# Spacing out the indirect row transfers at the hand-over from attention to the expert tiles

## The chip, the cores and the metric

The kernel runs on one core of a Trainium2 chip. The metric is the device time of one execution in microseconds; the kernel before was timed three times, and its median is the time before. One further execution was profiled, and all views below are of that one.

## The reference

Two layers follow each other. The first is attention over 4 batches of 8 heads, 768 positions and 64 features. Keys are grouped into 24 chunks of 32. For each query an upper bound of its score with every chunk is formed from the chunk's elementwise minimum and maximum, the six causal chunks with the highest bounds are kept, and a softmax attention runs over the kept, causal keys alone. The second layer sends each of the 3072 resulting rows of 512 numbers to one of eight experts:

```
ub    = sum_d max(q_d * kmin_d, q_d * kmax_d)        # per query and chunk, causal
keep  = the 6 chunks with the largest ub
attn  = softmax(scale * q k^T, kept and causal) v     # -> x, 3072 x 512
e     = argmax(x w_gate);  g = softmax(x w_gate)[e]
out   = g * (relu(x w1[e]) w2[e])                     # w1: 512 x 1024, w2: 1024 x 512
```

## The kernel before

**Attention, pairs 0 to 15.** Two heads are worked on at a time, which makes sixteen pairs (`NP = 16`), four to a batch. A pair has seven units: `scores(i, u)` makes the scores of unit u on TensorE (L469) and their exponentials on ScalarE (L474) into a tile P, and `av(i, u)` multiplies them with the values (L497). P tiles that cross the diagonal are masked, by GpSimd with an affine select (L482), in the last pair by VectorE with a product (L479). The pairs overlap: while pair i is in its scores, pair i+1 gets its chunk bounds (`ub`, `bound`, `maxes`, `choose`, `mask`, `put`) and pair i+2 its transposes. `norm(i, half)` divides a finished half by the softmax sums on VectorE (L521 to L525) and writes the row block `xrow` and the head's share `lgt` of the gate logits; `lg_add` sums these.

**Routing, once per batch.** When a batch's four pairs are done, `logits`, `gate`, `rank` (twelve small matmuls, L576 to L582) and `rank_v` find every row's expert and its slot `sli` among that expert's rows. Six indirect transfers of 128 rows each (`scatter`, L602) then write the rows to `xs_dram`, sorted by expert. For batches 0 to 2 this happens inside the next batch's pairs, at the slots that `scatters(i, slot)` lists; the last batch's six follow after attention has ended.

**Expert tiles.** 28 tiles of 128 rows are computed on the ordinary path, each for one expert. For tile j, `gather(j)` (L708) is an indirect transfer of its 128 rows from `xs_dram`; `x_in(j)` (L720) is a DMA transpose, issued by the SyncE queue, that puts them into the layout TensorE needs; `up(j)` is 8 matmuls (L741) followed by ReLU on ScalarE (L749) and a DMA transpose of the hidden rows, hT (L753), again on the SyncE queue; `down(j)` is 8 matmuls (L797), scaled on ScalarE (L803); and `y_out` (L781) is an indirect transfer of the 128 finished rows to their places in `out`. The first eleven tiles (`NA = 11`) hold rows of batches 0 to 2 alone, so their gathers may run before the last batch's rows are written. A table of tiles, `table(True)` for these eleven and `table(False)` for the others, comes from VectorE.

**Order.** The orders on TensorE, GpSimd and, after the first pair, VectorE are written out by hand (`manual_schedule`); in the tile phase the SyncE order is too. What is written first is executed first on its engine, and an instruction that waits holds back all behind it on that engine. In the last pair, `early` issues gathers as the pair goes on, each held back by a small GpSimd copy into `paced` that waits for a P tile:

```
if i == NP - 2 and slot == 3:
    gather(0)
    gather(1)
if i == NP - 1:
    if slot < 4:
        nc.gpsimd.tensor_copy(out=paced[:], in_=st[i][f"P{(1, 3, 5, 6)[slot]}"][0:1, 0, 0:1])
    gather(2 + slot)
    x_in(slot)
```

In the tile phase the order at step j is: at most one gather of a later tile, `up(j)` with its hidden transpose, at most one `x_in` of a later tile, then `down(j - 2)` with its output transfer. TensorE so runs up(j), down(j-2), up(j+1), down(j-1), and so on. From j = 8 on, the gather in step j is that of tile j+5 and the `x_in` that of tile j+3.

Of the kernel before, what the change touches and what calls it, by code (L numbers as in the profile page):

```python
# [10 lines left out]
FP32 = mybir.dt.float32  # L11
BF16 = mybir.dt.bfloat16
I32 = mybir.dt.int32
AF = mybir.ActivationFunctionType
# [10 lines left out]
def kernel(  # L25
# [10 lines left out]
    nc = tc.nc  # L36
# [4 lines left out]
    NCH = S // CH  # L41
# [58 lines left out]
    wgb = const.tile([128, HP, 2 * E], FP32)  # L100
    tokid = const.tile([128, B, 2, 3], I32)
    warm = const.tile([128, 1], FP32)
    paced = const.tile([1, 1], FP32)
    KTE, QSB, KS, KD = [], [], [], []
    for i in range(3):
        KTE.append(buf.tile([128, 2, S], BF16, name=f"KTE{i}"))
# [144 lines left out]
    def prep_steps(i):  # L251
# [120 lines left out]
        def select_first(filler, idle, scored, between):  # L372
            v_t(0)
            v_t(1)
            pm = [ps_m.tile([64, 384], BF16, tag="m", name="pm") for _ in range(2)]

            def turn(hf):
                for t in range(3):
                    nc.tensor.transpose(pm[hf][:, ts(t, 128)],
                                        nsel[:, 3 * hf + t].rearrange("p a n -> p (a n)"), ident_b[:])  # L380

            def put(hf):
                for hd in range(2):
                    nc.vector.tensor_copy(out=qsb[64:64 + NCH, hd, ts(hf, 384)],
                                          in_=pm[hf][32 * hd:32 * hd + NCH, :])

            bound()
            maxes(0, 3)
            choose(0, 3)
            turn(0)  # L390
            v_c(0, act=True)
            v_c(1, act=True)
            maxes(3, 6)
            choose(3, 6)
            put(0)
            filler()
            idle(2)
            scored()
            turn(1)
            between()  # L400
            put(1)
# [24 lines left out]
        def maxes(lo, hi):  # L426
            for t in range(lo, hi):
                for hd in range(2):
                    nc.vector.max(out=s["top8"][:, t, hd], in_=s["ubm"][:, t, hd])

        def choose(lo, hi):
            u3 = s["ubm"][:].rearrange("p t a n -> p (t a) n")[:, 2 * lo:2 * hi]
            t3 = s["top8"][:].rearrange("p t a n -> p (t a) n")[:, 2 * lo:2 * hi, TOPK - 1:TOPK]
            nc.vector.tensor_tensor(nsel[:].rearrange("p t a n -> p (t a) n")[:, 2 * lo:2 * hi, 0:NCH], u3,
                                    t3.to_broadcast([128, 2 * (hi - lo), NCH]), ALU.is_lt)
# [92 lines left out]
    def lg_add(i):  # L528
        b, hp = divmod(i, HP)
        eng = nc.vector if i == NP - 1 else nc.gpsimd  # L530
        lg, lgt = bst[b]["lg"], st[i]["lgt"]
        if hp == 0:
            eng.tensor_tensor(lg[:], lgt[:, :, :, 0], lgt[:, :, :, 1], ALU.add)
        else:
            for hd in range(2):
                eng.tensor_tensor(lg[:], lg[:], lgt[:, :, :, hd], ALU.add)
# [277 lines left out]
    def weights(slot):  # L814
        for n in range(2 * NW):
            if 1 + n * 71 // (2 * NW - 1) == slot:
                load_w(order_w[n // 2], n % 2)

    def scatters(i, slot):
        b, hp = divmod(i, HP)  # L820
        todo = {(1, 1): (0,), (1, 3): (2,), (2, 1): (4,), (2, 3): (1,), (3, 1): (3,), (3, 3): (5,)}
        if b == B - 1:
            todo = {(1, 1): (0, 2), (1, 2): (4, 1), (1, 3): (3, 5)}
        if b > 0 and (hp, slot) in todo:
            route[b - 1]["scatter"](todo[hp, slot])

    def early(i, slot):
        if i == NP - 2 and slot == 3:
            gather(0)
            gather(1)  # L830
        if i == NP - 1:
            if slot < 4:
                nc.gpsimd.tensor_copy(out=paced[:], in_=st[i][f"P{(1, 3, 5, 6)[slot]}"][0:1, 0, 0:1])
            gather(2 + slot)
            x_in(slot)

    MAN = {PE, POOL}
    with tc.manual_schedule(engines=MAN):
# [5 lines left out]
        with tc.manual_schedule(engines={DVE, ACT}):  # L844
            idle = consts_first()
            p0, p, pj = prep[0], prep[1], prep[2]
            p0["first"](idle)
            load(1, "v")
            spread(1, "k")
            load(2, "k")  # L850
            spread(1, "q")
            load(2, "q")
            load(2, "v")
            consts_pool()
            consts_last()
            idle(2)

            def filler():
                p["k_t"](0)
                idle(3)  # L860

            p0["select_first"](filler, idle, lambda: scores(0, 0), lambda: p["k_red"](0))
            scores(0, 1)
            p["k_t"](1)
            spread(2, "k")
            load(3, "k")
            p["k_out"](0, 0)
            p["k_out"](0, 1)
            p0["vw"]()
            p["k_red"](1)  # L870
            p0["vw_c"]()
            scores(0, 2)
            p["k_out"](1, 0)
            p["k_out"](1, 1)
            p["q_t"](0)
            p["q_t"](1)
            spread(2, "q")
            load(3, "q")
            av(0, 0)
            p["kse"]()  # L880
            p["q_va"](0)
            p["q_v"](1)
            p["q_a"](0)
            p["q_a"](1)
            scores(0, 3)
            av(0, 1)
            p["ub"]()
            norm(0, 0)
            p["bound"]()
            p["maxes"](0, 6)  # L890
            p["choose"](0, 6)
            scores(0, 4)
            av(0, 2)
            p["q_c"](0)
            p["q_c"](1)
            p["q_d"](0)
            p["q_d"](1)
            weights(1)
            pj["k_t"](0)
            pj["k_t"](1)  # L900
            spread(3, "k")
            load(4, "k")
            scores(0, 5)
            pj["k_red"](0)
            pj["k_out"](0, 0)
            pj["k_out"](0, 1)
            av(0, 3)
            p["mask"]()
            p["put"]()
            scores(0, 6)  # L910
            weights(2)
            weights(3)
            p["v_t"](0)
            p["v_t"](1)
            p["v_c"](0, act=True)
            pj["k_red"](1)
            p["v_c"](1)
            pj["k_out"](1, 0)
            pj["k_out"](1, 1)
            mask_rows(1)  # L920
            av(0, 4)
            pj["q_t"](0)
            pj["q_t"](1)
            spread(3, "q")
            load(4, "q")
            pj["q_va"](0)
            pj["q_v"](1)
            pj["kse"]()
            mask_rows(2)
            av(0, 5)  # L930
            pj["q_a"](0)
            pj["q_a"](1)
            pj["q_s"](0)
            weights(4)
        dve = tc.manual_schedule(engines={DVE})
        dve.__enter__()
        for i in range(1, NP):
# [10 lines left out]
            norm(i - 1, 1)  # L948
            load(i + 2, "v")
            lg_add(i - 1)  # L950
            if i < NP - 1:
                scores(i, 0)
                scores(i, 1)
# [7 lines left out]
                pn["q_s"](1)  # L961
            weights(5 * i)
            scatters(i, 0)
            early(i, 0)

            if pj:
                pj["k_t"](0)
# [11 lines left out]
            spread(i + 3, "k")  # L979
            load(i + 4, "k")  # L980
            weights(5 * i + 1)

            av(i, 0)
            scores(i, 3)
# [63 lines left out]
        norm(NP - 1, 1)  # L1048
        lg_add(NP - 1)
        with tc.manual_schedule(engines={SP, POOL}):  # L1050
            gather(7)
            x_in(5)
            r["logits"]()
            tok(0)
            tok(1)
            r["gate"]()
            gather(8)
            up(1)
            x_in(6)
            tok(2)  # L1060
            tok(3)
            r["rank"]()
            r["rank_v"]()
            gather(9)
            up(2)
            x_in(7)
            r["scatter"]((0, 1))
            gather(10)
            down(0)
            tok(4)  # L1070
            tok(5)
            for _ in table(False):
                pass

            def tiles(lo, hi):
                for j in range(lo, hi + 2):
                    if lo == 0 and j < 3:
                        continue
                    if lo == 0 and j < 5:
                        r["scatter"](((2, 3), (4, 5))[j - 3])  # L1080
                    if lo == 0 and 6 <= j < hi - 5:
                        gather(j + 5)
                    if j < hi:
                        up(j)
                    if lo == 0 and (j < 6 or 8 <= j < hi - 3):
                        x_in(j + (5 if j < 6 else 3))
                    if lo == 0 and j + 3 < hi:
                        tok(j + 3)
                    if lo == 0 and j == hi + 1:
                        down_last()  # L1090
                    elif j - 2 >= lo:
                        down(j - 2, turn_last if lo == 0 and j == hi else None)

            tiles(0, JM)
        dve.__exit__(None, None, None)
# [47 lines left out]
```

The softmax here doesn't subtract the row's maximum and nothing guards it: scores larger than these inputs give would overflow.

## Time and profile before

| what | value |
|---|---|
| device time, three runs | 345.01, 348.87, 351.6 us; median 348.87 us |
| span of the profiled execution | 353.5 us |
| TensorE busy | 324.1 us, 92% of the span |
| GpSimd busy | 211.2 us, 60% |
| ScalarE busy, VectorE busy | 206.6 us and 179.1 us |
| row scatters L602, mean of one | 1043 ns |
| output scatters L781, mean of one | about 989 ns |
| gathers L708, mean of one | about 1050 ns |

The shares are averages over phases with different limits. Attention takes the first 243 us of the profiled span, and the tile phase, with the last batch's routing inside it, the rest. The mean of an indirect transfer is the time for which GpSimd is occupied by it; the rows move afterwards, on the DMA engines. In the windows view, the columns after the stretch and its length are busy times of TensorE matmul, TensorE weight load, VectorE, ScalarE and GpSimd with their instruction counts, then the granted TensorE clock as a share of full speed, the DMA engines' busy share, and the bytes that they moved in GB/s.

### The profile page before, as it was taken

The numbers are of one execution on the slowest core, as the hardware profiler recorded it, in microseconds if no ns is written. First come the engines' busy times: TensorE is split into PE (matmuls) and PEld (weight loads), VectorE is DVE, ScalarE is ACT, GpSimd is POOL, SyncE is SP. The second block draws the span as 40 slices with busy tenths as digits, with TensorE's granted clock in tenths as the row PEclk, the third lists the DMA queues.
The fourth block names the chain that finished last, engine by engine and source line by source line (L and its number), as shares of the span: only waits on it lengthen the run. The fifth ranks groups of instructions, "written<-read, shape, count | busy, mean of one in ns | idle before, by whom it ended". The sixth has DMA issues, their size and how long they took to land.

```text
span 353.5 us, 13417 instructions
## 1 busy us (share of the span) xinstructions
PE 324.1 (92%) x5333; PEld 241.7 (68%) x5333; DVE 179.1 (51%) x725; ACT 206.6 (58%) x353; POOL 211.2 (60%) x368
## 2 busy tenths in 40 slices
PE   7899988999999999999999969876999999999990
PEld 3589978989899998799898858662444444444440
DVE  7778675776975776965866946424600000000010
ACT  4677865966767867667867735431344544454540
POOL 8657364555487785597893585553655656554231
PEclk9999999999999999999999989997899999999997
DMA  8968979789799999799897766245899998998730
GB/s 183 222 144 165 242 139 189 151 168 198 161 176 222 204 179 216 150 186 223 161 222 111 130 125 119 54 99 120 179 196 228 213 209 191 210 205 173 202 95 23
DMA packets 107005, 59.93 MB, mean 170 GB/s; under 512 B 76219, under 2 KB 99773, under 8 KB 106944
## 3 DMA queue, kind: packets, MB, share of 16 engines
q0 software_dynamic: 18048, 29.42, 44.1%
q1 hardware_dynamic: 87296, 29.26, 38.0%
q8 instruction: 44, 0.72, 0.8%
q10 hardware_dynamic: 1600, 0.39, 0.5%
q14 instruction: 17, 0.14, 0.1%
HBM read 56.14 MB, written 10.51 MB: 189 GB/s over the span
## 4 chain that ended last, share of the span: by engine, by line
PE 62%; issue 11%; POOL 7%; DVE 6%; ACT 4%; DMA 3%; another core or an unknown queue 2%; SPq 1%; POOLq 0%; ACTq 0%; DVEq 0%
PE po L497 22%; PE ps L469 10%; PE ubp L416 6%; PE ph L741 5%; PE py L797 5%; POOL out_dram L781 3%; PE pt L259 3%; PE vwp L334 3%; PE pt L318 3%; PE pt L287 3%; ACT P L474 2%; DMA QSB<-xg 1%; DMA hT<-h__5430 1%; PE pm L440 1%
## 5 line engine op out<-in xcount | busy, mean ns | idle before, releaser
L474 ACT ACTIVATE P<-ps 128x768 f32<-128x768 f32 x144 | 88.0, 664 | 44.9 <-PE ps L469 35.4
L497 PE MATMUL po<-V,P 128*64 128x73 f32 x2688 | 106.1, 228 | 8.3 <-POOL P L482 2.9
L497 PEld LDWEIGHTS po<-V,P 128*64 128x64 f32 x2688 | 99.9, 137 | 16.2 <-issue 4.5
L469 PE MATMUL ps<-QSB,KTE 128*64 128x384 bf16 (+2 forms) x576 | 55.3, 296 | 0.6 <-ACT P L474 0.6
L482 POOL TENSOR_SCALAR_AFFINE_SELECT P<-P 128x256 f32<-128x256 f32 x90 | 34.6, 408 | 29.8 <-ACT P L474 29.4
L797 PE MATMUL py<-w_all,hT 128*128 x216 | 51.0, 379 | 0.5 <-DMA hT<-h__5430 0.5
L274 ACT ACTIVATE KTE<-pt 64x512 bf16<-64x512 f32 (+1 forms) x64 | 31.0, 485 | 22.9 <-DVE kmn L270 22.1
L199 POOL DMA_DIRECT2D w_all<-in_moe_w_dram x64 | 41.3, 646 | 0.1
L797 PEld LDWEIGHTS <-hT 128*128 128x128 bf16 x216 | 21.1, 98 | 26.1 <-DMA hT<-h__5430 0.9
L469 PEld LDWEIGHTS <-KTE 128*64 128x64 bf16 x576 | 28.7, 111 | 6.9 <-issue 5.8
L602 POOL DMA_INDIRECT xs_dram<-xrow,sli x21 | 21.9, 1043 | 18.9 <-DVE xrow L568 7.7
L741 PE MATMUL ph<-w_all,KTE 128*128 x120 | 31.1, 403 | 2.0 <-issue 1.9
L781 POOL DMA_INDIRECT out_dram<-V,ti x14 | 13.8, 989 | 18.4 <-ACT V L803 15.4
L741 PE MATMUL ph<-w_all,QSB 128*128 x104 | 24.6, 379 | 0.0
L416 PE MATMUL ubp<-KS,qT 128*64 128x48 f32 x384 | 24.1, 224 | 0.2
L741 PEld LDWEIGHTS <-KTE 128*128 128x128 bf16 x120 | 12.0, 101 | 17.9 <-issue 5.9
L416 PE MATMUL ubp<-KD,qA 128*64 128x48 f32 x384 | 23.7, 222 | 0.4 <-issue 0.4
L521 DVE RECIPROCAL rec<-po 128x6 f32<-128x6 f32 x32 | 6.2, 195 | 34.7 <-PE po L497 17.4
L416 PEld LDWEIGHTS ubp<-KS,qT 128*64 128x64 f32 x384 | 20.6, 137 | 3.1 <-PE pt L259 2.0
L444 DVE COPY QSB<-pm 24x768 bf16<-24x768 bf16 x30 | 16.5, 551 | 8.8 <-PE pm L440 8.1
L416 PEld LDWEIGHTS ubp<-KD,qA 128*64 128x64 f32 x384 | 20.5, 138 | 0.6 <-issue 0.6
L328 DVE COPY vT<-pt 128x384 f32<-128x384 f32 x29 | 15.9, 553 | 8.8 <-PE pt L318 8.7
(207 smaller groups left out, 503.5 us busy)
## 6 DMA issues: line engine op xcount, KB each, us to landing
w_all<-in_moe_w_dram POOLq DMA_DIRECT2D x64, 256.0 KB
V<-in_v_dram SPq DMA_DIRECT2D x32, 192.0 KB
w_all<-in_q_dram SPq DMA_DIRECT2D x30, 192.0 KB
k<-in_k_dram SPq DMA_DIRECT2D x15, 256.0 KB
k<-in_k_dram SPq DMA_DIRECT2D x15, 128.0 KB
xs_dram<-xrow,sli POOLq DMA_INDIRECT x21
out_dram<-V,ti POOLq DMA_INDIRECT x14
q<-in_q_dram ACTq DMA_DIRECT2D x2, 96.0 KB
```

The costliest lines, as they stand in the source:

```text
L199: d = nc.gpsimd.dma_start(out=dst, in_=src)
L274: nc.scalar.activation(kte[0:64, hd, ds(128 * lo, 128 * n)].rearrange("p (w s) -> p w s", s=n), s[f"kp{hf}"][64 * hd:64 * hd + 64, :].rear ...
L416: nc.tensor.matmul(pu[c:c + CW, 3 * hf + t].rearrange("p a n -> p (a n)"), lhsT=s[f"{nm}{hf}"][:, ds(t * 128 + c, CW)], rhs=w_[:], start=( ...
L444: nc.vector.tensor_copy(out=qsb[64:64 + NCH, hd, :], in_=s["pm"][32 * hd:32 * hd + NCH, :])
L469: nc.tensor.matmul(pv[c:c + CW, hd, :], lhsT=kte[:, hd, ds(kb * 128 + c, CW)], rhs=qsb[:, hd, ds(qb * 384 + 384 - w, w)], start=True, stop ...
L474: nc.scalar.activation(P[:, :, ds(c0, w)], pv, AF.Exp)
L482: nc.gpsimd.affine_select(out=pd, in_=pd, pattern=[[0, 2], [1, 128]], compare_op=ALU.is_ge, fill=0.0, base=0, channel_multiplier=-1)
L497: nc.tensor.matmul(po[c:c + CW, t].rearrange("p a d -> p (a d)")[:, ds(hd * VW, VW)], lhsT=P[:, hd, ds(col + c, CW)], rhs=vt[:, kb, ds((1 ...
L602: d = nc.gpsimd.indirect_dma_start(out=xs_dram[:], out_offset=bass.IndirectOffsetOnAxis(ap=sli[:, u:u + 1], axis=0), in_=bst[b][f"xrow{u % ...
L741: nc.tensor.matmul(ph[:, fh, :], lhsT=xT[:, c, :], rhs=w1_all[:, ds(wo + (c * F + fh * 512), 512)], start=(c == 0), stop=(c == NDC - 1), s ...
L781: d = nc.gpsimd.indirect_dma_start(out=out[:], out_offset=bass.IndirectOffsetOnAxis(ap=ti[:], axis=0), in_=y, in_offset=None, bounds_check ...
L797: nc.tensor.matmul(py[:], lhsT=hT[:, c, :], rhs=w2_all[:, ds(wo + c * DM, DM)], start=(c == 0), stop=(c == NFC - 1))
```

## The change

Indirect transfers on GpSimd are spread out so that in the written order at most two follow each other in the last three pairs and around the first tiles. What stands between them is other GpSimd work or, where there is none, memsets of a small tile (`rest_a_while`, three memsets of 1 x 256 numbers).

- The scatters of batch 2 go from two to a slot in pair 13 to one at each of six slots over pairs 13 and 14.
- `gather(0)` stays at the end of pair 14, `gather(1)` goes to the start of pair 15; the later early gathers are each held back by a copy (`behind`) that waits for a tile of pair 15, then a memset. `gather(6)` waits for the second half of pair 15's logits.
- After attention, gathers 6 and 7 come ahead of the last batch's scatters, gather 8 after the first output, gathers 9 and later in the steps j = 5 and on. So the gather of step j is that of tile j+4 (before: j+5), and `x_in` there is that of tile j+3 for j = 4 and 5 and of tile j+2 from j = 7 on (before: j+3 from j = 8 on).
- On TensorE `up(2)` moves ahead of the last batch's `rank`.
- Near the start, one of two mask copies of the first pair moves from VectorE to ScalarE, `put(0)` ahead of `choose(3, 6)`, and two filler matmuls are dropped; in the same prologue `av(0, 4)` and one reduction move ahead of the value transposes.

```
-    paced = const.tile([1, 1], FP32)
+    paced = const.tile([1, 256], FP32)
...
-                for hd in range(2):
-                    nc.vector.tensor_copy(out=qsb[64:64 + NCH, hd, ts(hf, 384)],
-                                          in_=pm[hf][32 * hd:32 * hd + NCH, :])
+                nc.vector.tensor_copy(out=qsb[64:64 + NCH, 0, ts(hf, 384)], in_=pm[hf][0:NCH, :])
+                nc.scalar.activation(qsb[64:64 + NCH, 1, ts(hf, 384)], pm[hf][32:32 + NCH, :], AF.Copy)
...
+            put(0)
             choose(3, 6)
-            put(0)
             filler()
-            idle(2)
+            idle(1)
...
         if b == B - 1:
-            todo = {(1, 1): (0, 2), (1, 2): (4, 1), (1, 3): (3, 5)}
+            todo = {(1, 1): (0,), (1, 2): (2,), (1, 3): (4,), (2, 0): (1,), (2, 1): (3,), (2, 2): (5,)}
...
+    def rest_a_while(n=3):
+        for _ in range(n):
+            nc.gpsimd.memset(paced[:], 0.0)
+
+    def behind(ap):
+        nc.gpsimd.tensor_copy(out=paced[:, 0:1], in_=ap)
+        rest_a_while(1)
+
     def early(i, slot):
         if i == NP - 2 and slot == 3:
+            rest_a_while(1)
             gather(0)
-            gather(1)
         if i == NP - 1:
+            s = st[i]
+            if slot == 0:
+                behind(s["P2"][0:1, 0, 0:1])
+            if slot == 1:
+                behind(s["lgt"][0:1, 0, 0, 0, 0:1])
+            if slot == 2:
+                behind(s["P5"][0:1, 0, 0:1])
+            if slot == 3:
+                behind(s["P6"][0:1, 0, 0:1])
             if slot < 4:
-                nc.gpsimd.tensor_copy(out=paced[:], in_=st[i][f"P{(1, 3, 5, 6)[slot]}"][0:1, 0, 0:1])
-            gather(2 + slot)
+                gather(2 + slot)
             x_in(slot)
...
-                idle(3)
+                idle(2)
...
+            av(0, 4)
+            pj["k_red"](1)
             p["v_t"](0)
             p["v_t"](1)
             p["v_c"](0, act=True)
-            pj["k_red"](1)
...
-            av(0, 4)
...
             lg_add(i - 1)
+            if i == NP - 1:
+                gather(1)
...
             scatters(i, 0)
-            early(i, 0)
...
             weights(5 * i + 1)
+            early(i, 0)
...
         with tc.manual_schedule(engines={SP, POOL}):
+            behind(st[NP - 1]["lgt"][0:1, 0, 1, 0, 0:1])
+            gather(6)
+            rest_a_while()
             gather(7)
+            rest_a_while()
             x_in(5)
             r["logits"]()
             tok(0)
             tok(1)
             r["gate"]()
-            gather(8)
             up(1)
             x_in(6)
             tok(2)
             tok(3)
+            up(2)
             r["rank"]()
             r["rank_v"]()
-            gather(9)
-            up(2)
-            x_in(7)
             r["scatter"]((0, 1))
-            gather(10)
+            rest_a_while()
             down(0)
             tok(4)
             tok(5)
+            gather(8)
+            rest_a_while()
...
                         r["scatter"](((2, 3), (4, 5))[j - 3])
-                    if lo == 0 and 6 <= j < hi - 5:
-                        gather(j + 5)
+                        rest_a_while()
+                    if lo == 0 and 5 <= j < hi - 4:
+                        gather(j + 4)
                     if j < hi:
                         up(j)
-                    if lo == 0 and (j < 6 or 8 <= j < hi - 3):
-                        x_in(j + (5 if j < 6 else 3))
-                    if lo == 0 and j + 3 < hi:
-                        tok(j + 3)
+                    if lo == 0 and (j in (4, 5) or 7 <= j < hi - 2):
+                        x_in(j + (3 if j < 6 else 2))
+                    if lo == 0 and (j < 6 or 7 <= j < hi - 2):
+                        tok(j + (3 if j < 6 else 2))
                     if lo == 0 and j == hi + 1:
                         down_last()
                     elif j - 2 >= lo:
                         down(j - 2, turn_last if lo == 0 and j == hi else None)
+                    if lo == 0 and j < 5:
+                        rest_a_while()
```

## The prediction

> **What bounds the kernel now.** I read the page's busy shares first, then the chain of waits, then the windows of the stages that it named, then each engine's timeline there.
>
> ```profile
> PE 324.1 (92%) x5333; PEld 241.7 (68%) x5333; DVE 179.1 (51%) x725; ACT 206.6 (58%) x353; POOL 211.2 (60%) x368
> ...
> PEclk9999999999999999999999989997899999999997
> ```
>
> TensorE is the bound, so only its pauses and slow clock can be won: 353.5 - 324.1 = 29 us idle. The clock dips in two slices. The chain has one step of unknown releaser, at the hand-over:
>
> ```profile
> 234.02 0.76 DVE P L479 x2
> 234.78 8.36 another core or an unknown queue
> 243.16 0.21 DVE rec L521
> ...
> 246.44 3.48 PE ph L741 x8
> 249.91 1.73 PE py L797 x8
> ...
> 291.08 4.28 DMA QSB<-xg
> ```
>
> The reciprocal at 243.16 needs the end of attention's products, which should come soon after 235. The timelines of TensorE and GpSimd show what lies between:
>
> ```profile
> 235.06 2.45 PE L497 MATMUL po<-V,P 128*64 128x73 f32 x59
> 237.83 0.36 PE L497 MATMUL po<-V,P 128*64 128x73 f32 x3 [0.33 <-issue]
> 238.54 0.38 PE L497 MATMUL po<-V,P 128*64 128x73 f32 x4 [0.35 <-issue]
> ```
> ```profile
> 235.69 1.02 POOL L708 DMA_INDIRECT xg<-xs_dram,grow  x1 [0.16 <-issue]
> 237.01 1.01 POOL L708 DMA_INDIRECT xg<-xs_dram,grow  x1 [0.30 <-issue]
> ...
> 239.63 1.00 POOL L708 DMA_INDIRECT more_x<-xs_dram,grow  x1 [0.30 <-issue]
> ```
>
> TensorE pauses with "issue", waiting for nothing visible, while six gathers follow each other on GpSimd from 234.15 on. Its 72 last products take 5.2 us (235.06 to 240.3), against 2.4 for the same 72 a pair earlier. The count reaches VectorE at 243.14, about when the row of gathers is over. I read this as the indirect transfers holding back TensorE's issue and its counts; it is a coincidence in time so far, not shown. The same signs are smaller elsewhere: two gathers at 222.85 and 224.26 (24 value products spread over 1.94 us, elsewhere 0.66), and the six of 252.65 to 259.06, after which a ScalarE step of tile 2 stood idle 3.81 us.
>
> The last phase has no slack:
>
> ```profile
> 268.00:289.00 21.00, 21.00 (x99) 9.50 (x97) 0.96 (x6) 9.93 (x13) 12.28 (x12) 1.00 1.00 214
> ```
>
> TensorE is busy all 21.00 us, and the DMA engines too (share 1.00). Eight matmuls of `up` or `down` take 1.73 us.
>
> **What the Trainium skill says.** "TensorE: Matmul & The Clock Gate", Part 1: after an idle window of about 3.4 us the clock halves until about 3.4 us of activity. The trace agrees: 0.50 in 243 to 249, where `up(2)` takes 3.48 instead of 1.73 us. "Perfetto Trace Analysis", DMA Instruction — SWDGE (GPSIMD): the instruction ends when its descriptors are written, not when data has moved. It agrees: a gather occupies GpSimd 1.0 us and lands about 3.3 after issue. "DMA: Bandwidth & Descriptors", Issuing engines are not separate DMA queues: all issuers share 16 engines[...]. No page I read says that indirect transfers in a row hold back TensorE.
>
> **The change part by part: gains.**
>
> *Start.* Two idle matmuls of 0.216 us go: -0.4. The split of the mask copies (0.5 us) over two engines is what lets them go, so I count it with them. `av(0, 4)` ahead of the value transposes only swaps TensorE's own work: nothing.
>
> *A, scatters of pair 13.*
>
> ```profile
> 209.30 1.73 PE L497 MATMUL po<-V,P 128*64 128x73 f32 x24 [2.67 <-POOL P L482]
> ```
>
> Its products wait 2.67 us at 209.30 for a GpSimd mask that stood behind two scatters (206.44, 207.80), and run at clock 0.50 in 209 to 212 (24 in 1.73). One scatter less ahead is 1.0 + 0.30 = 1.3; a shorter wait may keep the clock, 1.65 more at most. Taken -2.5, bounds 1.3 and 2.95. The three scatters moved to pair 14: two find GpSimd idle (3.79 us at 217 to 221); the last delays masks by 0.9, of which I count +0.2.
>
> *B, gathers 0 and 1 apart.* 1.94 - 0.66 = 1.3 at most; -1.0 (0.6 to 1.3).
>
> *C, the stutter at 235.* The next gathers have a copy and a memset between them. The memset's price isn't in the trace: 128x128 takes 0.21, 64x768 0.73, so 0.31 for 1x256 (0.21 to 0.36). If that suffices, the count comes at 235.06 + 2.4 = 237.5 instead of 243.14; the unknown is whether one such pause is enough. Of these 5.6 I take 5.2, since some pauses of 0.3 will stay beside single gathers (4 to 5.7). The added waits hold only gathers behind them on GpSimd, whose rows are needed after 243.
>
> *D, `up(2)` ahead of `rank`.* Before, 6.77 us pass from 243.14 to the first `down` (249.91), the slow `up(2)` among them. After: two `up` of 1.73, half a microsecond, 0.9 for the first hidden transpose: 4.9. So -1.9 (1 to 1.9).
>
> Gains: 0.4 + 2.5 - 0.2 + 1.0 + 5.2 + 1.9 = **10.8 us**.
>
> **Losses.**
>
> *E, gather 9 comes late.* Before, it went out ahead of the last scatters; now it stands behind six scatters, three outputs and gather 8: ten transfers of 1.0, gaps 5 x 0.30 + 6 x 0.16 (0.30 behind another transfer, 0.16 behind compute), six rests of 0.93, together 18.0. With 1.6 from `rank` to the first scatter, its landing of 3.3 and 3.2 for its `x_in` that is 26.1 after `rank`. `up(9)` is due 13 steps of 1.73 later, 22.5, plus the 0.9 that the first hidden transpose cost in D: 2.7 late. Taken +2.9, since its `x_in` also queues on SyncE (1 to 4). What waits behind it on TensorE is everything: `down(7)` follows `up(9)` in the written order.
>
> *F, the row moves.* From step 5 on gathers 9 to 12 and the outputs between go back to back again, seven transfers, while the tiles run with less slack. Counts came up to 3.1 late in the row of six before. +1.0 (0 to 4).
>
> *G, `x_in` two tiles ahead.* ScalarE and SyncE queues for one tile:
>
> ```profile
> 274.74 1.02 ACT L749 ACTIVATE h__5568<-ph 128x1024 bf16<-128x1024 f32 x1 [0.99 <-PE ph L741]
> ```
> ```profile
> 275.79 1.28 SPq L753 DMA_TRANSPOSE hT<-h__5568  x1
> 277.18 1.21 SPq L720 DMA_TRANSPOSE KTE<-KTE  x1
> ```
>
> `x_in` stands behind the hidden transpose on SyncE, so it is issued 2.5 us after the end of `up(j)`. Before it was for tile j+3, now for j+2. Between the end of `up(j)` and `up(j+2)` lie three steps, 5.18 us, so landing may take 5.18 - 2.5 - 0.1 = 2.6. It took 2.4 to 6.2 in 268 to 302, median 3.2. What is over 2.6 is lost once per two tiles, nine times in the 18 tiles from 9 on. A pause thins the traffic, so I choose L = 3.0, between shortest and median: 0.4 x 9 = +3.6. At 2.7 it is 0.9, at 3.2 5.4, at 3.4 7.2, at 3.6 9.0.
>
> Losses: 2.9 + 1.0 + 3.6 = 7.5. **Net -3.3: 348.87 - 3.3 = 345.6 us.**
>
> **The rivals.**
>
> *R2, full gain.* Landing shortens as soon as TensorE waits, or E and G fall together (a late gather 9 moves all later needs), so little is given back: 348.87 - 10.8 = 338.1, with all gains at their ends about 336. For it: landing has a wide spread and many x come early. Against: DMA share 1.00.
>
> *R3, slower.* The lead is too short: E 2.9, F 4 (a row of seven with no slack), G 7.2 (L = 3.4), 14.1 in all; the gains at their lower ends 0.4 + 1.3 - 0.4 + 0.6 + 4.0 + 1.0 = 6.9. 348.87 + 7.2 = 356.1. For it: TensorE's 21.00 of 21.00 leaves nothing to absorb it; median landing is above 2.6.
>
> *R4, no stutter to win.* The profiled span is 353.5, the median run 348.87: part of the long stall may be of that execution only, or one memset is too short a pause. Without C: -5.6 + 7.5 = +1.9, 350.8. For it: the mechanism is only inferred. Against: the smaller cases of it at 202, 222 and 252 too.
>
> **How the numbers follow.** Forecast 0.45, R2 0.28, R3 0.15, R4 0.12. 2% lies at 341.9 and 355.8. Faster: R2, and a quarter of the forecast's spread (G at 2.7): 0.39. Slower: most of R3 and a little of the others: 0.16. Within: 0.45. The range runs from R2's far end, 336, to R3's 356.
>
> **What would show it.** A and C right: the wait at 209 falls to about 1.3 with the clock full, and the chain has no step near 8 us of unknown releaser; wrong if TensorE still pauses with "issue" between the spaced gathers. E: `up(9)` idles on the DMA of its x for about 3 us. G: in the last phase TensorE is no longer busy 21 of 21, with short idles ahead of L741, released by x, on every other tile. R2: the last phase stays at 1.00. R3: idles above 0.8 us per two tiles, or a clock of 0.50 there. The prediction is wrong if the sum of these idles is far from 4 to 7 us, or if the end of attention does not move by about 8 us.

## The result, and the profile after

The changed kernel is slower: 371.47 us (median of four executions, 365.6 to 373.64) against 347.81 us for the kernel before in the same comparison (345.01 to 351.6). The ratio is 1.060, with a 95% interval of 1.040 to 1.079. Here and below the ratio compares the executions within 1.5% of their kernel's fastest, and the medians are over all executions. So the loss is some 21 us by the ratio and 24 by the medians.

The first view is the page of the profile after, its busy shares and the clock in 40 slices. TensorE did the same work, 325.4 us of it, in a span of 367.8 us instead of 353.5. So the idle time grew, from 29 to 42 us. The slices of slow clock now lie in the tile phase.

```profile
PE 325.4 (88%) x5331; PEld 240.3 (65%) x5331; DVE 178.4 (49%) x723; ACT 207.6 (56%) x355; POOL 220.0 (60%) x399
...
PEclk9999999999999999999999999969969999899997
```

TensorE's timeline shows attention end sooner than in the trace of before, as the prediction had it. (Lines have moved: L496 are the attention products, L740 is `up`, L796 is `down`; in brackets stands the idle time before and what ended it.)

```profile
207.83 0.98 PE L496 MATMUL po<-V,P 128*64 128x73 f32 x24 [1.60 <-POOL P L481]
...
231.19 2.52 PE L496 MATMUL po<-V,P 128*64 128x73 f32 x72
...
241.45 3.57 PE L796 MATMUL py<-w_all,hT 128*128 x8 [3.90 <-DMA hT<-h__5130]
...
264.54 1.89 PE L796 MATMUL py<-w_all,hT 128*128 x8
...
279.52 1.89 PE L796 MATMUL py<-w_all,hT 128*128 x8
```

The wait of pair 13 is 1.60 instead of 2.67 us and its 24 products run at full clock (0.98 instead of 1.73 us). The last 72 products take 2.52 us, with no pauses. The last reciprocal starts 9.4 us sooner than in the trace of before. But the first `down` then waits 3.90 us for its hidden rows and runs at half clock: 3.57 us for eight matmuls instead of 1.89. The last two lines are `down(6)` and `down(8)`, which are needed further down.

From there on the time is lost. From the first `down` to the end of the span the changed kernel takes 126.4 us, the kernel before 103.7. This is the chain of waits, in order of time ("issue" is time in which nothing visible is waited for):

```profile
236.76 4.57 DMA hT<-h__5130
241.33 0.13 issue
241.45 3.57 PE py L796 x8
...
262.35 4.08 DMA more_x<-xs_dram,grow
266.45 3.73 DMA QSB<-more_x
```

The last two lines are gather 9 and its `x_in`: `up(9)` stands behind both. The same stop and three later ones on TensorE's timeline, and a window of 21 us in the last phase, to set beside the 21.00 of 21.00 of the kernel before (its TensorE column is the first after the length):

```profile
271.78 3.57 PE L740 MATMUL ph<-w_all,QSB 128*128 x8 [5.34 <-DMA QSB<-more_x]
275.14 2.81 PE L796 MATMUL py<-w_all,hT 128*128 x8
...
285.63 1.89 PE L740 MATMUL ph<-w_all,KTE 128*128 x8 [0.77 <-ACT KTE L802]
...
294.88 1.89 PE L740 MATMUL ph<-w_all,KTE 128*128 x8 [2.08 <-DMA KTE<-spare]
...
316.75 2.42 PE L740 MATMUL ph<-w_all,KTE 128*128 x8 [2.04 <-DMA KTE<-more_x]
318.96 3.09 PE L796 MATMUL py<-w_all,hT 128*128 x8
```
```profile
278.00:299.00 21.00, 18.15 (x84) 8.02 (x83) 0.80 (x5) 8.97 (x11) 10.16 (x10) 1.00 0.73 171
```

TensorE is busy 18.15 of 21.00 us, and the DMA engines' share has fallen from 1.00 to 0.73. So the DMA engines had room left, and the transposes were asked for too late. After `up(9)` the trace has nine such idles ahead of an `up`, on about every other tile (12, 14, 16, 18, 19, 22, 24, 25 and 27), 0.6 to 2.1 us each, 10.6 us in all. (Some of them carry the name of another engine that was done earlier, as that of 285.63; the transpose of its rows landed last, at 285.10.)

### The profile page after: what moved, and what is told of

Same layout as the page of the kernel before. It is cut to its first block, busy times and chain, and to the rows that moved or that the text cites. A ratio compares the mean times of both kernels' runs of the same rounds, so it can differ in the third digit from the quotient of the medians.

```text
span 367.8 us, 13437 instructions
## 1 busy us (share of the span) xinstructions
PE 325.4 (88%) x5331; PEld 240.3 (65%) x5331; DVE 178.4 (49%) x723; ACT 207.6 (56%) x355; POOL 220.0 (60%) x399
## 4 chain that ended last, share of the span: by engine, by line
PE 45%; issue 19%; POOL 13%; DMA 9%; ACT 7%; DVE 4%; POOLq 1%; SPq 1%; DVEq 0%; ACTq 0%
PE po L496 17%; PE ps L468 8%; PE ubp L415 5%; POOL out_dram L780 4%; ACT P L473 3%; DMA more_x<-xs_dram,grow 3%; PE pt L259 3%; PE pt L287 3%; PE vwp L334 2%; PE pt L318 2%; PE py L796 2%; POOL xg L707 2%; ACT KTE L274 2%; POOL xs_dram L601 1%; DMA hT<-h__5130 1%
## 5 line engine op out<-in xcount | busy, mean ns | idle before, releaser
L496 PE MATMUL po<-V,P 128*64 128x73 f32 x2688 | 104.2, 227 | 5.8 <-POOL P L481 1.8
L496 PEld LDWEIGHTS po<-V,P 128*64 128x64 f32 x2688 | 98.7, 136 | 13.4 <-PE ps L468 3.1
L796 PE MATMUL py<-w_all,hT 128*128 x216 | 54.8, 400 | 3.9 <-DMA hT<-h__5130 3.9
L468 PE MATMUL ps<-QSB,KTE 128*64 128x384 bf16 (+2 forms) x576 | 54.4, 293 | 0.6 <-ACT P L473 0.6
L796 PEld LDWEIGHTS <-hT 128*128 128x128 bf16 x216 | 22.1, 102 | 32.0 <-issue 5.5
L740 PE MATMUL ph<-w_all,KTE 128*128 x120 | 28.7, 384 | 7.9 <-DMA KTE<-spare 2.6
L740 PE MATMUL ph<-w_all,QSB 128*128 x104 | 27.0, 406 | 8.4 <-DMA QSB<-more_x 5.3
L468 PEld LDWEIGHTS <-KTE 128*64 128x64 bf16 x576 | 27.9, 109 | 6.8 <-issue 5.8
L740 PEld LDWEIGHTS <-KTE 128*128 128x128 bf16 x120 | 11.6, 97 | 23.1 <-issue 3.8
L740 PEld LDWEIGHTS <-QSB 128*128 128x128 bf16 x104 | 10.7, 103 | 23.1 <-issue 5.5
L415 PEld LDWEIGHTS ubp<-KS,qT 128*64 128x64 f32 x384 | 19.6, 137 | 2.6 <-PE pt L259 1.7
L328 DVE COPY vT<-pt 128x384 f32<-128x384 f32 x29 | 15.9, 552 | 10.6 <-PE pt L318 10.6
```

Of the source, the lines that this page charges most:

```text
L415: nc.tensor.matmul(pu[c:c + CW, 3 * hf + t].rearrange("p a n -> p (a n)"), lhsT=s[f"{nm}{hf}"][:, ds(t * 128 + c, CW)], rhs=w_[:], start=( ...
L468: nc.tensor.matmul(pv[c:c + CW, hd, :], lhsT=kte[:, hd, ds(kb * 128 + c, CW)], rhs=qsb[:, hd, ds(qb * 384 + 384 - w, w)], start=True, stop ...
L496: nc.tensor.matmul(po[c:c + CW, t].rearrange("p a d -> p (a d)")[:, ds(hd * VW, VW)], lhsT=P[:, hd, ds(col + c, CW)], rhs=vt[:, kb, ds((1 ...
L740: nc.tensor.matmul(ph[:, fh, :], lhsT=xT[:, c, :], rhs=w1_all[:, ds(wo + (c * F + fh * 512), 512)], start=(c == 0), stop=(c == NDC - 1), s ...
L796: nc.tensor.matmul(py[:], lhsT=hT[:, c, :], rhs=w2_all[:, ds(wo + c * DM, DM)], start=(c == 0), stop=(c == NFC - 1))
```

## The experiments

All kernels below compute the whole reference. Each was timed with the kernel before on the same chip, and the ratio is to that. The median of the kernel before was 348 to 349 us on most chips, and 357 to 358 us on the two chips of e10 and e11.

| kernel | median us | ratio to before | 95% interval |
|---|---|---|---|
| changed kernel | 371.47 | 1.060 | 1.040 to 1.079 |
| e7, tile order alone | 371.13 | 1.067 | 1.060 to 1.075 |
| e1, attention alone | 350.22 | 0.996 | 0.991 to 1.001 |
| e2, lead of three again | 355.60 | 1.018 | 1.010 to 1.026 |
| e9, lead of two alone | 364.27 | 1.036 | 1.027 to 1.045 |
| e3, gathers 8 to 10 early | 367.41 | 1.054 | 1.044 to 1.064 |
| e5, no rests in the tile phase | 367.30 | 1.056 | 1.050 to 1.063 |
| e4, first hidden transpose first | 369.82 | 1.061 | 1.053 to 1.069 |
| e6, e1 with that transpose first | 348.62 | 0.998 | 0.994 to 1.001 |
| e8, e1 with the transposes between | 347.18 | 0.995 | 0.992 to 0.998 |
| e10, scatters alone | 355.04 | 0.988 | 0.980 to 0.995 |
| e11, e1 on another chip | 354.06 | 0.987 | 0.975 to 1.000 |

**Which half loses.** e1 has the changed attention and, from the last `lg_add` on, the order of before; e7 is the reverse. The edit that makes e1 out of the changed kernel, cut to its core:

```
             gather(6)
-            rest_a_while()
             gather(7)
-            rest_a_while()
             x_in(5)
...
+            gather(9)
+            up(2)
+            x_in(7)
             r["scatter"]((0, 1))
-            rest_a_while()
+            gather(10)
             down(0)
...
-                    if lo == 0 and 5 <= j < hi - 4:
-                        gather(j + 4)
+                    if lo == 0 and 6 <= j < hi - 5:
+                        gather(j + 5)
...
-                    if lo == 0 and (j in (4, 5) or 7 <= j < hi - 2):
-                        x_in(j + (3 if j < 6 else 2))
+                    if lo == 0 and (j < 6 or 8 <= j < hi - 3):
+                        x_in(j + (5 if j < 6 else 3))
```

> The changed kernel's attention with the order of the kernel before from the last `lg_add` on. Order theory (all of the loss lies in the order of the tile phase, attention itself gained 9.4 us by its last reciprocal): 338 to 341 us, about 8 below the kernel before, TensorE busy near 100% from the tenth tile on. Rival (spacing the early gathers makes the first tiles late, whatever follows): some of the gain is lost at the first `down`, 343 to 350 us. Rival (the long stall belongs to single executions): 347 us.

> The kernel before with nothing changed but the order from the last `lg_add` on, which is that of the changed kernel. If the order of the tile phase is the whole of the loss and spacing in attention gained nothing that a timed run sees (0.4% in the attention-alone run): 370 us, as the changed kernel. If spacing gained some 5 us that the order gives back elsewhere: 375 us or more. If the loss needs both (the spaced gathers come late and the short lead makes it felt): 360 us or less.

e7 has the whole loss (1.067, an interval that overlaps that of the changed kernel) and e1 none of it (0.996; by the medians of all executions 1.006). So the order of the tile phase is the loss, and on e1's chip the new attention can't be told from no change in time. Where what e1 won went is seen in its chain of waits, with the same place on TensorE's timeline in e7 below it:

```profile
238.39 5.55 DMA hT<-h__5130
243.94 0.13 issue
244.06 3.15 PE py L796 x8
```
```profile
241.28 3.24 PE L797 MATMUL py<-w_all,hT 128*128 x8 [3.73 <-DMA hT<-h__5127]
```

In e1 the first hidden transpose is issued at 238.39, behind two `x_in` that wait for spaced gathers; the first `down` waits 3.13 us for it and starts at half clock. The first rival of its expectation, early tiles made late by the spacing, was right in part. The hidden rows are ready 4.3 us before the issue in e1 and 4.4 in the changed kernel, and 2.3 to 3.1 in b_again, b_again2 and e7, where the gathers stand in a row. So this transpose stood behind two `x_in` before too, and the spacing added 1 to 2 us. In e7 the first `down` waits 3.73 us without spaced gathers; there the transpose took 5.65 us to land.

**The lead of `x_in`.** e2 puts back, in the changed kernel, gathers five tiles ahead from step 6 on and `x_in` three ahead from step 8 on. e9 changes one thing in the kernel before: from tile 11 on, `x_in` goes out one hidden transpose later, and with it `tok`, a small VectorE operation on the same rows.

```
-                    if lo == 0 and (j < 6 or 8 <= j < hi - 3):
-                        x_in(j + (5 if j < 6 else 3))
+                    if lo == 0 and (j < 6 or 9 <= j < hi - 2):
+                        x_in(j + (5 if j < 6 else 2))
```

> The changed kernel, but from step 8 on `x_in` is three tiles ahead and gathers five, as before; gather 9 stays late. Lead theory (an x transpose issued two tiles ahead lands 0.5 to 2 us late on every other tile, 10.6 us of idle and 1.8 us of slow clock in the trace): 12 us less than the changed kernel, 359 us. Rival (the idles come from transfers that land later whatever the lead, or from GpSimd's row of gathers and outputs): less than 4 us, 367 us or more.

> The kernel before with one thing changed: from tile 11 on its `x_in` is issued one hidden transpose later on SyncE, so that it is two tiles ahead instead of three. Lead theory (2.4 us to issue, at least 2.9 to land, 0.5 from landing to the first matmul, against 5.0 us that three steps give): up(11) and every later one is late, 13.6 us in all by the trace of the changed kernel, 361 us. Rival (the short lead costs only beside the late gathers and the rests): 352 us or less.

Both fit the lead theory. By the ratios e2 wins 4.1 points of the 6.0, about 14 us where 12 were expected; e9 loses 3.6 points (12.6 us of 348; interval 9 to 16; 15.5 by the medians) with nothing else changed. First the window of e2 in the last phase, then that of e9 (the profiled execution of e9 took 369 us, above its median, so it serves for the pattern, not for the size):

```profile
283.00:304.00 21.00, 20.89 (x97) 9.47 (x97) 0.99 (x6) 10.55 (x13) 12.17 (x12) 1.00 1.04 212
```
```profile
278.00:299.00 21.00, 17.13 (x77) 7.52 (x77) 0.96 (x6) 8.03 (x10) 10.22 (x10) 1.00 0.73 174
```

With three tiles TensorE is busy 20.89 of 21.00; with two, 17.13. How long the loop is can be read from one tile in the changed kernel, tile 11 on ScalarE and then on SyncE:

```profile
283.18 1.02 ACT L748 ACTIVATE h__5661<-ph 128x1024 bf16<-128x1024 f32 x1 [0.99 <-PE ph L740]
```
```profile
284.22 1.23 SPq L752 DMA_TRANSPOSE hT<-h__5661  x1
285.55 1.23 SPq L719 DMA_TRANSPOSE KTE<-spare  x1
```

`up(11)` ends at 283.14. The `x_in` of tile 13 is issued at 285.55, 2.41 us later. By its completion counts in the trace it has landed at 288.66, after 3.11 us, and `up(13)` starts at 289.19, 0.53 us after that: 6.05 us in all. Three steps of TensorE give 5.02 (3 x 1.73, less the 0.16 by which the last matmul's record overlaps the next).

The 0.53 us are not the transfer's. TensorE loads the expert's weight offset `woff` into a register (L733) for each `up`, and this load begins only when the rows have landed, here at 288.70, and takes 0.30 us:

```profile
L733 PEldq TENSOR_LOAD <-woff x17: 299/302/686, 280.3 to 349.9; - x17
```

The line gives the count, the shortest, median and longest load in ns, and the first and last start, for tiles 11 to 27. A `down` has no such load, and `down(0)` starts 0.13 us after its hidden rows have landed, in the changed kernel and in e1 (the "issue" lines above). Whether the load could run ahead of the wait was not tried. This is what the view of the `x_in` line says of all `x_in` from 276 us on, in the changed kernel:

```profile
  PEld L740: 9.8, 9
  PE ph L740: 6.0, 5
...
DMA to landing us min/median/max: 2.5/3.0/5.1
```

The first two lines are who waited for them (us, times). The landing would have to be 5.02 - 2.41 - 0.53 = 2.1 us, and the quickest took 2.5. So no `x_in` could come in time while TensorE ran without a stop. A stop at one tile gives the next one room, which is why the idles stand on about every other tile. In e2 the landings were 3.0 to 4.1 us at a DMA share of 1.04, and nothing waited, since three tiles give 8.47 us.

**Gather 9.** e3 issues gathers 8 and 9 right after gather 7 and gather 10 behind the first scatters; e5 takes out the rests and keeps the order.

```
             gather(7)
             rest_a_while()
+            gather(8)
+            gather(9)
...
-                    if lo == 0 and 5 <= j < hi - 4:
+                    if lo == 0 and 7 <= j < hi - 4:
```

> The changed kernel, but gathers 8 and 9 are issued right after gather 7 and gather 10 after the first two scatters, as early as before; the lead of two stays. Late-gather theory (`up(9)` idles 5.3 us and the clock then runs at half for 2.9 us more, because gather 9 stands behind everything on GpSimd): that stop goes, 7 us less than the changed kernel, 364 us, and the losses on every other tile stay. Rival (with a lead of two the stop only moves to the next tile, or TensorE's counts come late beside the longer row): 2 us or less, 369 us or more.

> The changed kernel without the memset rests from the last `lg_add` on, the order kept. If the rests are what makes gather 9 late (six of about 1 us ahead of it): it is issued some 5 us sooner, the stop at `up(9)` shrinks, 4 us less than the changed kernel, 367 us. If its place in the order is: within 1.5 us of the changed kernel.

By time neither can be told from the changed kernel with certainty: 4 us less by the medians, 1 to 2 by the ratios, with overlapping intervals. By the ratios both rivals would stand, so the time decides nothing here. The traces say where the rest stays. From `down(6)` to `down(8)` the changed kernel takes 15.0 us, the kernel before 6.9 (the first two lines below); e3 takes 11.3 and e5 11.3 (the other two).

```profile
271.09 1.89 PE L797 MATMUL py<-w_all,hT 128*128 x8
...
277.99 1.89 PE L797 MATMUL py<-w_all,hT 128*128 x8
```
```profile
265.17 1.89 PE L796 MATMUL py<-w_all,hT 128*128 x8
269.60 2.81 PE L740 MATMUL ph<-w_all,QSB 128*128 x8 [2.54 <-issue]
...
276.46 1.89 PE L796 MATMUL py<-w_all,hT 128*128 x8
```

In e5 gather 9 is issued at 256.19 instead of 262.35; its order is that of the changed kernel and only the rests are gone. So about 3.7 us of that stop come from the lateness of gather 9, and the rests are enough of a reason for it. Some 4.4 us remain: 2.5 of idle and 1.7 of half clock behind it. They belong to the lead. In e3 the rows of gather 9 have landed at 247.6, but `x_in(9)` is issued only behind hidden transpose 7, at 262.82; it lands at 267.50, and `up(9)` starts at 268.22. In e1, with the gather as early and the longer lead, `x_in(9)` is issued at 255.34 and nothing stops. The late-gather theory had put all of the stop down to the gather. Of the rivals in the two expectations, the one of e5 (the place in the order alone) doesn't fit the trace.

**The first hidden transpose.** e4 issues it ahead of `x_in(3)` to `x_in(5)` in the changed kernel, e6 does so in e1, and e8, also from e1, orders SyncE as hidden 0, x 3, hidden 1, x 4, x 5, hidden 2, and so on with `x_in` four tiles ahead up to step 6 (e1: five). The edit of e4:

```
-            x_in(slot)
+            if slot < 3:
+                x_in(slot)
...
+                sp = tc.manual_schedule(engines={SP})
+                sp.__enter__()
                 up(0)
...
+            x_in(3)
+            x_in(4)
             x_in(5)
             r["logits"]()
```

> The changed kernel, but the first hidden transpose is issued ahead of `x_in(3)` to `x_in(5)` on SyncE, which is all that moves. Queue theory (the first `down` waits 3.9 us at half clock afterwards, because the hidden transpose stands behind two `x_in` that wait for the spaced gathers): `down(0)` starts near 237.5 instead of 241.5 and at full clock, 5 us less than the changed kernel, 366 us. Rival (the time won there is lost again at `up(9)`, whose rows come no sooner): within 2 us of the changed kernel, with a longer wait at `up(9)`.

> The attention-alone kernel, but the first hidden transpose is issued ahead of `x_in(3)` to `x_in(5)` on SyncE. There the first `down` waited 3.1 us for this transpose and ran at half clock for 2.1 us more, and with a lead of three nothing later is late. Queue theory: both go, 4 to 5 us less than the attention-alone kernel, 344 us, 2% or less below the kernel before. Rival (`x_in(3)` to `x_in(5)` then come late for up(3), or the landing is slow whatever the order): within 1.5 us of the attention-alone kernel.

> The attention-alone kernel with SyncE's order at the first tiles made hidden 0, x 3, hidden 1, x 4, x 5, hidden 2, and so on. With hidden 0 alone put first the wait only moved to the second `down` (2.5 us and slow clock). Queue theory: now no `down` waits over 1 us for its hidden transpose, the 3 us that the spaced scatters and gathers won in attention stay won, 344 to 345 us against 348 of the kernel before. Rival (the landing is slow beside the row of gathers and scatters whatever SyncE's order): a wait of 2 us or more at one of the first three `down`, 347 us or more.

In e4 `down(0)` starts at 238.8 instead of 241.5, yet the time is the same (1.061): what is won there is spent at the second `down`, which waits 3.10 us, and in a stop at `up(9)` of 8.06 us instead of 5.34. The rival was right. In e6 `down(0)` comes at 241.6, but the wait moves one tile on:

```profile
247.70 2.42 PE L796 MATMUL py<-w_all,hT 128*128 x7 [2.51 <-DMA hT<-h__5231]
```

The second hidden transpose now stood behind `x_in(4)` and `x_in(5)`. e8 mends that too, and none of its first three `down` shows a wait for its hidden rows. So e8 is faster than both the kernel before (by 0.5%, interval 0.2 to 0.8) and the changed kernel. Against the kernel before that is 1.7 us, less than the 3 to 4 expected.

**The long stall.** Did the kernel before always stall for eight microseconds at the end of attention? These are two further executions of it, unchanged, and two kernels on chips where the kernel before took 357 us: e10, with spaced scatters alone and the row of gathers kept, and e11, which is e1 again.

```
-            todo = {(1, 1): (0, 2), (1, 2): (4, 1), (1, 3): (3, 5)}
+            todo = {(1, 1): (0,), (1, 2): (2,), (1, 3): (4,), (2, 0): (1,), (2, 1): (3,), (2, 2): (5,)}
```

> The kernel before, unchanged, looked at once more. Stall theory (six gathers in a row hold TensorE back in every execution): the step before the last reciprocal is again about 8 us, and the first `down` starts near 250. Rival (the long stall belonged to the one execution that was profiled, which took 355.3 us against a median of 348): the 72 last products take about 2.4 us, the step is below 4 us, the first `down` starts near 244.

> The kernel before, a further execution, since one look can't tell a habit from a chance: as for the other look, 8 us and 250 for the stall theory, below 4 us and 244 for the rival.

> The kernel before with one part of the change alone: batch 2's scatters go one to a slot over pairs 13 and 14. The wait at pair 13's mask (2.7 us and a slow clock) shrinks in the trace by about 2.1 us in every kernel that has this part. If that time reaches the end: 346 us, ratio about 0.994. If it is used up at the first tiles, as in the attention-alone kernel: ratio 0.998 to 1.002.

> The attention-alone kernel once more, because the long stall seems to belong to some chips: on the chip of the scatters-alone run the kernel before took 357.6 us and TensorE paused beside the row of six gathers, on the others it took 348 to 349 us and didn't pause. Spacing theory: on a chip of the first kind the stall goes and the ratio is near 0.98; on one of the second kind the ratio is again 0.99 to 1.00. Rival (spacing doesn't prevent the pauses): TensorE pauses with issue between 228 and 243 us here too where the chip is of the first kind.

b_again took 348.09 us and b_again2 351.74. The first line is from the chain of waits of b_again, with its row of gathers; the others are TensorE's timeline of e10, with the same row, and of e11, with the spaced one:

```profile
234.01 2.46 PE po L497 x72
```
```profile
236.54 0.22 PE L497 MATMUL po<-V,P 128*64 128x73 f32 x1 [0.38 <-issue]
237.26 0.52 PE L497 MATMUL po<-V,P 128*64 128x73 f32 x3 [0.49 <-issue]
238.70 0.41 PE L497 MATMUL po<-V,P 128*64 128x73 f32 x3 [0.92 <-issue]
```
```profile
235.11 2.51 PE L496 MATMUL po<-V,P 128*64 128x73 f32 x72
```

In b_again the row of gathers does nothing to TensorE: 72 products in 2.46 us (in b_again2, with the same row, 2.47, and in e9 2.52 by the timeline; in e7, whose row is broken by a rest, 2.47). The first `down` comes at 241.63 there, not near 250. In e10 TensorE pauses with "issue" beside the row, as in the profile that the prediction read, and its 72 products spread over 9 us. In e11, on another chip with slow times, the spaced gathers leave no pause. So six gathers in a row don't stall TensorE in every execution: two of the five with that row did. Whether the stall goes with the chip or with the single execution is not shown: the first execution that stalled stood beside timings of 345 to 352 us, not of 357, and there is no second trace from e10's chip. Nor is it shown that spacing prevents it, since e11's chip may not stall at all. What it is worth in time stays open: e10, which keeps the stall, and e11, which doesn't, stand at 0.988 and 0.987, from two chips, and from the first `down` to the end e11 took 109.9 us against 106.7 in e10. e10 is faster than the kernel before (0.980 to 0.995), which fits the 0.994 expected if the gain reaches the end.

## Why the prediction was wrong

The forecast was 345.6 us and the upper end of the range 356.0; the kernel took 371.5. The mechanisms of the loss were those of the rival R3; two of them, G and E, were about three times the size that the forecast gave them.

- **G was mis-sized, and it is the largest term.** The mechanism was right. The prediction took 0.1 us from landing to the first matmul and 5.18 us of room, and so a break-even landing of 2.6 us, which some transfers would meet; the loss was put at 3.6 us. A start 0.1 us after landing fits a `down` (0.13 measured) and not an `up`, which has the register load ahead of it: 0.53. The room was 5.02, so break-even was 2.1 us and no landing met it. The choice L = 3.0 was right as a median. But the loss follows the mean, 3.2 us with single landings of 4.4 to 5.1, since an early landing gives little back. Measured: 10.6 us of idle and some 2 us of slow clock in the trace, 12.6 us in e9, 14 us in e2.
- **E failed in size**: 2.9 predicted, 8.1 in the trace between `down(6)` and `down(8)`. Gather 9 went out 24.9 us after `rank`, where 19.6 was worked out: the first scatter began 3.9 us after `rank` instead of 1.6, since gather 7 and its rest stood ahead of it, a rest of three memsets took 1.02 us instead of 0.93, and GpSimd waited for outputs that were themselves late. About half of the excess was left out of the sum: an idle of 5.3 us drops the clock, and the next sixteen matmuls cost 2.6 us more. That is what the Trainium skill's "TensorE: Matmul & The Clock Gate", Part 1, says of an idle window of about 3.4 us, and the trace agrees with 3.57 us for eight matmuls after the stop. The prediction used it for the gain and not for the loss. But the traces don't bear out that a stop has to be that long. The clock halved after 2.04 us at `up(19)` in the changed kernel and after 2.67 in the trace of before (at 209.30), and not after 2.08 us at `up(14)` or 3.10 in e4. Ahead of the slow spell from 243 on that the prediction named, no single pause was over 0.9 us.
- **D failed.** `up(2)` ahead of `rank` was to win 1.9 us, with a wait of 0.9 for the first hidden transpose. The wait was 3.9 us plus slow clock. The prediction had overlooked that on SyncE this transpose stands behind `x_in(3)` and `x_in(4)`. They wait for gathers, which the change spaces out, and that added 1 to 2 us; e7, with these gathers in a row, waits 3.7 us all the same. Why the transpose lands only after 4.6 to 5.7 us there stays open. What an added wait on GpSimd holds back is not only on GpSimd. e4 shows that this cost nothing in the end, as `up(9)` stopped everything anyway.
- **C was no gain to count on.** The stall of 5.6 us was in the profiled execution, of 355.3 us against a median of 348.9, and not in b_again, b_again2, e7 or e9. The rival R4 said so, and the number that spoke for it stood in the table. That the end of attention moved by the 8 us or more that the prediction asked for was luck: the last reciprocal came at 233.75 us in the changed kernel and at 233.76 in e7, which has the attention of before. Executions differ by more than the change: the first value product of pair 11 came at 168.0 us in e7, 170.2 in the changed kernel and 177.2 in e9.
- **A was right, and B was not.** The last wait of pair 13 shortened and its clock stayed full. From the first value product of pair 13 to that of pair 14 pass 14.3 us in every kernel with spaced scatters, e10 among them, and 17.3 to 17.4 in the trace of before, b_again, e7 and e9 (16.6 in b_again2). So the scatters won 3.0 us, where 2.3 were forecast. From pair 14 to pair 15 the kernels don't differ, 11.6 to 11.7 us with gathers 0 and 1 in a row or apart, but for 12.05 in the one profile that the prediction read. The value products that B wanted to bring together took 0.88 us in b_again with both gathers in a row: nothing to win there.
- **F, late counts beside the new row of seven, was not tried by itself.** No wait of the traces needs it.

So the lead took about 13 us at the later tiles, and the stop at `up(9)` with its clock about 8, of which 4.4 are the lead's too; that makes the 21 of the ratio. The 3 us that attention won were used up at the first tiles.

The reading of the bandwidth was right in direction and too hopeful in size. I took a lower L because stalls thin the traffic, in the sense of "DMA: Bandwidth & Descriptors", Issuing engines are not separate DMA queues. From 276 us on the median landing was 3.0 us in the changed kernel and in e9, 3.1 in e2, and 3.4 and 3.9 in b_again and b_again2. But even the quickest, 2.5 us, was over the 2.1 that the loop left. The same page, Anatomy of one DMA, states a fixed part for transfers that GpSimd issues: about 2.0 us, most of it the write's confirmation. The quickest of these transposes from SyncE lies above it; whether they have such a part was not measured.

## What to carry to other kernels

Before a prefetch is moved one tile later, add up its whole loop: the end of the work that frees its place in the queue, every instruction ahead of it there, the mean landing (not the quickest), and the time from landing to the first use, with whatever the engine does only then (here a register load). If the room isn't larger than that sum, each tile is late, and no bandwidth helps. And a long stall in one profile is worth counting only if further executions show it too.

## What was not expected of the hardware

- Between a transpose's last completion count and the first matmul of an `up` that waited for it lie 0.53 us at the least (tiles 13, 14, 18, 25, 26 and 27 of the changed kernel), 0.30 of them for a register load that starts at the landing; ahead of `down(0)` it was 0.13 us.
- The slow spells of TensorE's clock in these traces last 3.4 or 6.8 us, and stops of 2 to 3 us brought some of them on and others not: 2.04 us did and 2.08 did not in the changed kernel.
- Pauses of TensorE beside a row of indirect transfers were there in two executions and absent in three, with the same GpSimd order there. On the two chips of e10 and e11 the kernel before takes 2.5% longer than on the rest.
- TensorE also pauses with no indirect transfer near: 1.8 us before 46.2 and 1.1 us before 92.8 in e1, at places that differ from one execution to the next.
